# Tile 0's second product four blocks at a time, loads in order of first use, one more pair of chunks through the DMA crossbar

## The chip, the cores and the metric

The kernel runs on one core of one Trainium2 chip. The metric is the device time of one execution in microseconds (us). A core has five engines that run side by side, each through its own instructions in order: TensorE (PE) multiplies matrices into PSUM, VectorE (DVE) and ScalarE (ACT) work element by element, GpSimd (POOL) also does element work and here issues all loads, and SyncE (SP) issues stores and transposing DMAs. They wait for each other through semaphores.

## The reference

A linear attention with decay feeds a two-layer network with an ELU between its layers. Sizes: batch 4, 8 heads, sequence 768, head size 64; so x is 3072 x 512, w_in 512 x 2048, w_out 2048 x 512. Cut to what is computed:

```python
for b in range(nb):                      # blocks of 64 positions
    intra = (einsum(qb, kb) * Dmask) @ vb          # decay lam ** (i - j), i >= j
    inter = (qb * lam_pow) @ kv_state
    out[:, :, sl] = intra + inter
    kv_state = lam_block * kv_state + einsum(kb * rev_pow, vb)
x = out.transpose(0, 2, 1, 3).reshape(B * S, H * D)
h = x @ w_in
g = where(h > 0, h, exp(min(h, 0)) - 1)
return (g @ w_out).astype(float32)
```

## The kernel before

It works in chunks of 128 positions of one batch (24 chunks, numbered 0 to 23; 0 to 3 are the first positions of the four batches and have no state). Chunks come in pairs; each pair passes through three visits: transposes of q and k (`att_T`, on PE through PSUM with a copy by ACT, or `att_xT`, by a transposing DMA, the crossbar), scores and mask (`att_S`, `att_mask`), outputs and state (`att_O`, `att_U`, `att_X`, `att_st`). Chunks are gathered to seven tiles, of 4, 2, 4, 4, 4, 4 and 2 chunks, whose columns go through the network: `mm1` makes one of 16 blocks of 128 hidden units (PE into psH), ACT makes e and r of it, DVE makes g (`elu`), and `mm2` adds one hidden block's part to one output block of 128 rows (PE into psM).

```python
TS = [4, 2, 4, 4, 4, 4, 2]                 # chunks of each tile

LOADS = [(0, 1, 'q'), (0, 1, 'k'), (0, 1, 'v'), (1, 1, 'q'), ...,
         (2, 1, 'v'), (3, 1, 'v'), ('wi', 0), ('wi', 1), ('wi', 2), ...,
         ('kd', 0), ('wi', 6), ('kd', 2), ('wo', 0), (4, 2), ('wo', 1), ('wo', 2), ('wo', 3),
         (6, 2), (8, 2), (10, 2), ..., (22, 2)]      # issued by POOL, in this order

def att_T(g, n, which, tag="S"):           # transposes on PE
    ...
            nc.tensor.transpose(pt[:, i, hp, :], in_=nat[:, 2 * hp : 2 * hp + 2, :],
                                identity=ident16[:])

def att_xT(g):                             # transposes by DMA, issued by SP
    for j, ts in enumerate((qn, kn)):
        dst = asb.tile([128, 2 * HP, 128], FP16, tag=f"{w}T", name=f"{w}T{g}", bufs=3)
        nc.sync.dma_start_transpose(out=dst[:], in_=heads(ts, g, 2)...)

def att_st(g):
    ...
        if c == 0:
            copy = nc.scalar.copy if g in (2,) else nc.vector.tensor_copy
            copy(out=new[r, :, :, r], in_=pu[r])

def mm1(t, n, alt=False):                  # psH: 2 buffers of tag H (and M for tile 0, some n)
    ...
    e = msb.tile([128, MT], FP32, tag="e", bufs=3, ...)
    nc.scalar.activation(e[:], pH[:], AF.Exp)
    r = msb.tile([128, MT], FP16, tag="r", bufs=3, ...)
    nc.scalar.activation(r[:], pH[:], AF.Relu)

def mm2(t, i, n, tag="M"):                 # psM: 2 buffers of tag M; copied and stored at n = 15
    ...
    nc.tensor.matmul(pm[:], lhsT=gt[t][:, n, i * L : (i + 1) * L],
                     rhs=wo_t[...], start=(n == 0), stop=(n == NF - 1))
    ...
    nc.sync.dma_start(out=out[t0 : t0 + L, :], in_=o[:])
```

The order of all this is written out by hand. A list of steps says which hidden block is made in a step and which (tile, output block, hidden block) parts of mm2 follow it; visits of the attention are attached to steps. Within a step, mm1 comes first, then what is attached, then g, then mm2. Stage A is tile 0's 16 hidden blocks, stage B steps without a hidden block; later steps carry their tile and hidden block, and E is the end.

```python
steps = [(('A', 0), (0, 0), []), ..., (('A', 9), (0, 9), []),
         (('A', 10), (0, 10), [(0, 0, 0), (0, 1, 0)]), ...,
         (('B', 0), None, [(0, 0, 6), (0, 1, 6), (0, 0, 7), (0, 1, 7)]), ... to ('B', 4),
         ((1, 0), (1, 0), [(0, 2, 0), (0, 3, 0), (0, 2, 1), (0, 3, 1)]), ...,
         ((2, 0), (2, 0), [(1, 0, 0), (1, 0, 1)]), ...]
for s, m1, m2 in steps:
    if m1 is not None:
        t, n = m1
        er = mm1(t, n, alt=t == 0 and n in (2, 4, 6))
    do(s)                                  # what is attached to this step
    if er:
        elu(t, n, *er)
    for t2, i2, n2 in m2:
        mm2(t2, i2, n2, "H" if t2 == 0 and m1 is None and i2 > 1 else "M")
```

At the start, `warm(k)` puts k matmuls of 512 columns without use on PE between the first transposes.

Of the kernel before, what the change touches and what calls it, by code (L numbers as in the profile page):

```python
# [7 lines left out]
FP32 = mybir.dt.float32  # L8
FP16 = mybir.dt.float16
I32 = mybir.dt.int32  # L10
AF = mybir.ActivationFunctionType
# [4 lines left out]
def kernel(  # L16
# [10 lines left out]
    nc = tc.nc  # L27

    B, H, S, D = q.shape
    L = 128  # L30
    HP = H // 2
# [6 lines left out]
    T0 = [sum(TS[:t]) for t in range(len(TS))]  # L38
# [74 lines left out]
    LOADS = [(0, 1, 'q'), (0, 1, 'k'), (0, 1, 'v'), (1, 1, 'q'), (1, 1, 'k'), (1, 1, 'v'), (2, 1, 'q'), (2, 1, 'k'), (3, 1, 'q'), (3, 1, 'k'), (2, 1, 'v'), (3, 1, 'v'), ('wi', 0), ('wi', 1), ('wi', 2), ('wi', 3), ('wi', 4), ('wi', 5), ('kd', 0), ('wi', 6), ('kd', 2), ('wo', 0), (4, 2), ('wo', 1), ('wo', 2), ('wo', 3), (6, 2), (8, 2), (10, 2), (12, 2), (14, 2), (16, 2), (18, 2), (20, 2), (22, 2)]  # L113

    def run_loads(items):
        for it in items:
            if it[0] == "wi":
                emit_wi(it[1])
            elif it[0] == "wo":
                emit_wo(it[1])  # L120
            elif it[0] == "kd":
                att_kd(it[1], 2, "p")
            else:
                emit_load(*it)

    nc.gpsimd.iota(rel_i[:], pattern=[[1, 128]], base=0, channel_multiplier=-1)
    run_loads(LOADS[:17])
# [31 lines left out]
    for hh in range(2):  # L159
        nc.vector.tensor_tensor(  # L160
            out=mask1[:, hh],
# [20 lines left out]

    def late_up():
        nc.scalar.activation(ks[:], loglam[:], AF.Exp, scale=pos[:, 1:2])
        for hh in range(2):
            r = slice(hh * 64, (hh + 1) * 64)
            nc.scalar.copy(loglam_p[r, :], loglam[r, hh::2])
        nc.scalar.activation(up_p[:], loglam_p[:], AF.Exp, scale=float(L))

    def late_qs(lo, hi):  # L190
        for hp in range(lo, hi):
            nc.scalar.activation(
                qs[:, hp, :], row[:], AF.Exp, scale=loglam_p[:, hp : hp + 1]
            )
# [105 lines left out]
    def att_S(g, tag="S"):  # L300
        s = ps.tile([128, 2, HP, 128], FP32, tag=tag, bufs=2, name=f"psS{g}")
        for hp in range(HP):
            for hh in range(2):
                r = slice(hh * 64, (hh + 1) * 64)
                nc.tensor.matmul(  # L305
                    s[:, hh, hp, :], lhsT=kT[g][r, hp, :], rhs=qT[g][r, hp, :],
                    start=True, stop=True,
                )
        pS[g] = s
# [37 lines left out]
    def att_X(g, n, parts=1):  # L347
        t, i = where[g]
        if i == 0:
            xt[t] = asb.tile([128, HP, TS[t] * L], FP16, tag="xt", name=f"xt{t}")  # L350
        po = pS.pop(("O", g))
        w = HP // parts
        for j in range(parts):
            c = slice(j * w, (j + 1) * w)
            dst = xt[t][:, c, i * L : (i + n) * L].rearrange("p h (n l) -> p n h l", n=n)
            if g < B:
                copy = nc.vector.tensor_copy if g == 0 else nc.scalar.copy
                copy(out=dst, in_=po[:, :, c])
                continue
            nc.vector.tensor_tensor(  # L360
                out=dst, in0=po[:, :, c],
                in1=qs[:, c].unsqueeze(1).broadcast_to([128, n, w, 128]),
                op=ALU.mult,
            )
# [36 lines left out]
    def att_st(g):  # L401
        c, b = divmod(g, B)
        if c == NC - 1:
            return
        pu = pS.pop(("U", g))
        new = st[b // 2][(c + 1) % 2]
        for hh in range(2):
            r = slice(hh * 64, (hh + 1) * 64)
            if c == 0:
                copy = nc.scalar.copy if g in (2,) else nc.vector.tensor_copy  # L410
                copy(out=new[r, :, :, r], in_=pu[r])
            else:
                nc.vector.tensor_tensor(  # L413
                    out=new[r, :, :, r], in0=tmps[g][r], in1=pu[r], op=ALU.add
                )
        tmps.pop(g, None)
# [18 lines left out]
    def mm1(t, n, alt=False):  # L435

        MT = TS[t] * L
        if MT == 256:
            if n == 0:
                gt[t] = msb.tile([128, NF, MT], FP16, tag="g", bufs=2, name=f"g{t}")  # L440
            pH = ps.tile([128, 2 * MT], FP32, tag="H", bufs=2, name=f"psH{t}_{n}")
            for x in range(2):
                wi, j = wi_t[wi_at[n + x][0]], wi_at[n + x][1]
                for kk in range(HP):
                    nc.tensor.matmul(  # L445
                        pH[:, x * MT : (x + 1) * MT],
                        lhsT=wi[:, kk, j * 128 : (j + 1) * 128],
                        rhs=xt[t][:, kk, :], start=(kk == 0), stop=(kk == HP - 1),
                    )
            MT *= 2  # L450
        else:
            if (t, n) not in pH_of:
                mm1_mm(t, n, 0, MT, "M" if t == 0 and n % 2 == 0 and n < 8 else "H")
            pH = pH_of.pop((t, n))
        e = msb.tile([128, MT], FP32, tag="e", bufs=3, name=f"e{t}_{n}")
        nc.scalar.activation(e[:], pH[:], AF.Exp)  # L456
        if alt:
            return e, None, pH
        r = msb.tile([128, MT], FP16, tag="r", bufs=3, name=f"r{t}_{n}")
        nc.scalar.activation(r[:], pH[:], AF.Relu)  # L460
        return e, r, pH
# [35 lines left out]
    def mm2(t, i, n, tag="M"):  # L497
        if T0[t] + i == NG - 1:
            if n == NF - 1:
                mm2_last(t, i)  # L500
            return
        if n == 0:
            psM[t, i] = ps.tile([128, DM], FP32, tag=tag, bufs=2, name=f"psM{t}_{i}")
        pm = psM[t, i]
        nc.tensor.matmul(  # L505
            pm[:], lhsT=gt[t][:, n, i * L : (i + 1) * L],
            rhs=wo_t[wo_at[n][0]][:, wo_at[n][1], :], start=(n == 0), stop=(n == NF - 1),
        )
        if n < NF - 1:
            return  # L510
        c, b = divmod(T0[t] + i, B)
        t0 = b * S + c * L
        o = msb.tile([128, DM], FP32, tag="osb", bufs=3, name=f"osb{t}_{i}")
        last = T0[t] + i == NG - 1
        if last:
            raise AssertionError
        else:
            if i % 2:
                nc.vector.tensor_copy(o[:], pm[:])
            else:  # L520
                nc.scalar.copy(o[:], pm[:])  # L521
            nc.sync.dma_start(out=out[t0 : t0 + L, :], in_=o[:])
        psM.pop((t, i))

    def warm(k, tag="M"):
        if k <= 0:
            return
        pw = ps.tile([128, 4, 128], FP32, tag=tag, bufs=2, name=f"psW{len(warms)}")
        warms.append(pw)
        for _ in range(k):  # L530
            nc.tensor.matmul(
                pw[:], lhsT=ident16[:], rhs=any16, start=True, stop=True
            )
# [13 lines left out]
    def op_T(c, w):  # L547
        att_T(c, 1, w, "H")

    def op_Te(c, w):  # L550
        att_Te(c, 1, w, "a")

    W = [5, 2, 3, 0, 1, 1, 0, 0, 1, 1, 0]
# [7 lines left out]
    late_up()  # L561
    warm(W[2])
    att_S(0)
    att_mask(0, 2)
    warm(W[3])
    op_T(1, "q")
    op_Te(1, "q")
    warm(W[4])
    op_T(1, "k")
    op_Te(1, "k")  # L570
    att_O(0, 1, "M")
    att_X(0, 1)
    warm(W[5])
    att_S(1)
    att_mask(1, 2)
    op_T(2, "q")
    op_Te(2, "q")
    warm(W[6])
    op_T(2, "k")
    op_Te(2, "k")  # L580
    warm(W[7])
# [3 lines left out]
    att_mask(2, 2)  # L585
    att_O(1, 1, "M")
    att_X(1, 1)
    warm(W[8])
    att_T2(3, "k", "H")
    warm(W[9])  # L590
    att_S(3)
    att_mask(3, 2)
    att_O(2, 1, "M")
    att_X(2, 1)
    late_qs(0, 2)
    warm(W[10])
    for n in range(0):
        mm1_mm(0, n, 0, 3 * L, "MH"[n % 2])
    att_OX2(3, "H")
    for n in range(0, 1):  # L600
        mm1_mm(0, n, 0, 3 * L, "MH"[n % 2])
    late_qs(2, HP)
    for n in range(1):
        mm1_mm(0, n, 3 * L, 4 * L)

    run_loads(LOADS[17:27])
# [8 lines left out]
    XT = {10: (1, 12), 12: (2, 4), 14: (2, 12), 16: (3, 4), 18: (3, 12), 20: (4, 4), 22: (4, 12)}  # L615
# [23 lines left out]
    for g, vs in [(4, (('A', 12), ('A', 14), ('B', 1))), (6, ((1, 0), (1, 4), (1, 6))), (8, ((1, 8), (1, 12), (1, 14))), (10, ((2, 0), (2, 2), (2, 5))), (12, ((2, 8), (2, 10), (2, 13))), (14, ((3, 0), (3, 2), (3, 5))), (16, ((3, 8), (3, 10), (3, 13))), (18, ((4, 0), (4, 2), (4, 5))), (20, ((4, 8), (4, 10), (4, 13))), (22, ((5, 0), (5, 2), (5, 5)))]:  # L639
        visit(g, *vs)  # L640
    for s, a, b in [((1, 0), 27, 28), ((1, 4), 28, 29), ((1, 8), 29, 30), ((1, 12), 30, 31), ((2, 0), 31, 32), ((2, 3), 32, 33), ((2, 6), 33, 34), ((2, 9), 34, 35)]:
        at(s, run_loads, LOADS[a:b])

# [42 lines left out]
```

## Time and profile before

| | |
|---|---|
| Time, median of 3 runs | 216.54 us (216.33 to 216.77) |
| Span of the profiled run | 215.2 us |
| PE busy | 203.1 us, 94% |
| DVE busy | 151.0 us, 70% |
| ACT busy | 127.8 us, 59% |
| POOL busy | 79.0 us, 37% |
| DMA of loads (POOL's queue) | 13.63 MB |
| DMA of stores and transposes (SP's queue) | 9.90 MB |

Busy time of an engine is the time in which at least one of its instructions runs, and an idle piece before an instruction is put down to what released it. Matmuls overlap in the records, so a busy PE is not one at its peak: beside the busy time, the time from start to start of the same matmuls has to be read. DMA records give the time of each transfer's issue and of its landing.

### The profile page before, as it was taken

The numbers are of one execution on the slowest core, as the hardware profiler recorded it, in microseconds if no ns is written. First come the engines' busy times: TensorE is split into PE (matmuls) and PEld (weight loads), VectorE is DVE, ScalarE is ACT, GpSimd is POOL, SyncE is SP. The second block draws the span as 40 slices with busy tenths as digits, with TensorE's granted clock in tenths as the row PEclk, the third lists the DMA queues.
The fourth block names the chain that finished last, engine by engine and source line by source line (L and its number), as shares of the span: only waits on it lengthen the run. The fifth ranks groups of instructions, "written<-read, shape, count | busy, mean of one in ns | idle before, by whom it ended". The sixth has DMA issues, their size and how long they took to land.

```text
span 215.2 us, 4091 instructions
## 1 busy us (share of the span) xinstructions
PE 203.1 (94%) x1650; PEld 105.9 (49%) x1650; DVE 151.0 (70%) x193; ACT 127.8 (59%) x241; POOL 79.0 (37%) x76
## 2 busy tenths in 40 slices
PE   4977979899999999999999999999999999999994
PEld 1443434566764544544544545545445444555543
DVE  6666998985999999997887786766565543423221
ACT  6848888436566766676565566466456567454510
POOL 8999958469498948255400000000000000000000
DMA  6999999999999999999992413314211011111112
GB/s 40 146 157 169 206 171 195 191 162 150 157 126 156 206 138 168 135 156 177 184 153 74 75 49 86 63 49 98 53 49 52 0 49 49 53 49 49 49 51 99
DMA packets 98756, 23.87 MB, mean 111 GB/s; under 512 B 90928, under 2 KB 95792, under 8 KB 98736
## 3 DMA queue, kind: packets, MB, share of 16 engines
q0 software_dynamic: 80208, 13.63, 84.1%
q1 hardware_dynamic: 18384, 9.90, 21.6%
q8 instruction: 13, 0.21, 0.4%
q10 hardware_dynamic: 144, 0.07, 0.1%
q14 instruction: 7, 0.06, 0.1%
HBM read 27.27 MB, written 6.29 MB: 156 GB/s over the span
## 4 chain that ended last, share of the span: by engine, by line
PE 58%; POOL 17%; DMA 14%; issue 5%; DVE 4%; ACT 0%; POOLq 0%; DVEq 0%
PE psM L505 29%; PE psH L430 15%; PE psH L445 6%; DMA kT<-kn 5%; DMA qn<-in_q_dram 5%; DMA wo<-in_moe_w_out_dram 4%; POOL qn L72 3%; POOL kn L72 3%; POOL vn L72 3%; POOL tmp L394 3%; POOL wi L97 2%; DVE g L473 2%; PE psO L331 2%; POOL kd L292 2%; PE psM L485 2%
## 5 line engine op out<-in xcount | busy, mean ns | idle before, releaser
L473 DVE SCALAR_TENSOR_TENSOR g<-e,r 128x512 f16<-128x512 f32 x93 | 69.5, 761 | 41.7 <-ACT r L460 41.2
L456 ACT ACTIVATE e<-psH 128x512 f32<-128x512 f32 x96 | 57.5, 599 | 63.9 <-PE psH L430 48.4
L505 PE MATMUL psM<-wo,g 128*128 128x512 f16 x368 | 93.9, 380 | 1.0 <-DMA wo<-in_moe_w_out_dram 0.9
L430 PE MATMUL psH<-xt,wi 128*128 128x512 f16 (+2 forms) x324 | 81.2, 377 | 1.2 <-DMA wi<-in_moe_w_in_dram 0.8
L460 ACT ACTIVATE r<-psH 128x512 f16<-128x512 f32 x93 | 55.3, 595 | 0.0
L505 PEld LDWEIGHTS <-g 128*128 128x128 f16 x368 | 34.2, 98 | 38.7 <-DMA wo<-in_moe_w_out_dram 1.4
L430 PEld LDWEIGHTS <-wi 128*128 128x128 f16 x324 | 31.1, 98 | 38.9 <-DMA wi<-in_moe_w_in_dram 1.3
L317 DVE TENSOR_TENSOR P<-psS,mask 128x1024 f16<-128x1024 f32 (+1 forms) x28 | 28.7, 1066 | 4.0 <-PE psS L305 3.8
L394 POOL TENSOR_TENSOR tmp<-st,up_p 64x512 f32<-64x512 f16 x16 | 21.4, 1336 | 13.3 <-DVE st L413 12.5
L72 POOL DMA_DIRECT2D qn<-in_q_dram x14 | 15.8, 1125 | 5.1 <-issue 4.5
L72 POOL DMA_DIRECT2D vn<-in_v_dram x14 | 15.3, 1096 | 5.9 <-issue 4.9
L445 PE MATMUL psH<-xt,wi 128*128 128x256 f16 x128 | 16.6, 273 | 0.0
L72 POOL DMA_DIRECT2D kn<-in_k_dram x14 | 15.3, 1092 | 3.0 <-issue 1.8
L360 DVE TENSOR_TENSOR xt<-psO,qs 128x1024 f16<-128x1024 f32 x10 | 12.2, 1221 | 4.9 <-PE psO L339 4.7
L445 PEld LDWEIGHTS <-wi 128*128 128x128 f16 x128 | 12.5, 98 | 4.9
L521 ACT COPY osb<-psM 128x512 f32<-128x512 f32 x12 | 7.1, 590 | 11.8 <-PE psM L505 11.8
L331 PE MATMUL psO<-P,vn 128*64 128x128 f16 x184 | 11.9, 223 | 0.8 <-DVE P L317 0.8
L292 DVE TENSOR_TENSOR kd<-kn,ks 128x1024 f16<-128x1024 f16 x8 | 12.4, 1549 | 0.0
L331 PEld LDWEIGHTS <-vn 128*64 128x64 f16 x184 | 9.6, 109 | 5.1 <-issue 4.4
L413 DVE TENSOR_TENSOR st<-tmp,psU 64x512 f16<-64x512 f32 x16 | 10.9, 679 | 0.2
L339 PE MATMUL psO<-qT,st 128*64 128x128 f16 x160 | 10.2, 219 | 0.0
L305 PE MATMUL psS<-qT,kT 64*128 64x128 f16 x192 | 8.2, 221 | 0.9 <-DMA kT<-kn 0.7
(62 smaller groups left out, 106.4 us busy)
## 6 DMA issues: line engine op xcount, KB each, us to landing
out_dram<-osb SPq DMA_DIRECT2D x23, 256.0 KB, 2.3
qn<-in_q_dram POOLq DMA_DIRECT2D x10, 256.0 KB, 12.2
kn<-in_k_dram POOLq DMA_DIRECT2D x10, 256.0 KB, 14.8
vn<-in_v_dram POOLq DMA_DIRECT2D x10, 256.0 KB, 15.7
wo<-in_moe_w_out_dram POOLq DMA_DIRECT2D x4, 512.0 KB, 13.6
wi<-in_moe_w_in_dram POOLq DMA_DIRECT2D x2, 512.0 KB, 9.6
wi<-in_moe_w_in_dram POOLq DMA_DIRECT2D x3, 256.0 KB, 7.3
qn<-in_q_dram POOLq DMA_DIRECT2D x4, 128.0 KB, 4.5
```

What stands on the lines that cost most here:

```text
L72: nc.gpsimd.dma_start(out=dst, in_=src[b : b + n, :, rows].rearrange("b h p d -> p (b h) d"))
L292: e.tensor_tensor(out=kd[:].rearrange("p (n h) d -> p n h d", n=n), in0=heads(kn, g, n).rearrange("p (n h) d -> p n h d", n=n), in1=ks_b, ...
L317: nc.vector.tensor_tensor(out=P[:, :, c], in0=s[:, :, c], in1=(mask if g < B else mask1)[:, :, c], op=ALU.mult,)
L331: nc.tensor.matmul(po[r, i, hp, :], lhsT=v_of(g + i, 2 * hp + hh), rhs=P[:, hh, hp, :], start=True, stop=(c == 0), skip_group_check=True,)
L360: nc.vector.tensor_tensor(out=dst, in0=po[:, :, c], in1=qs[:, c].unsqueeze(1).broadcast_to([128, n, w, 128]), op=ALU.mult,)
L394: e.tensor_tensor(out=tmp[r], in0=old[r, :, :, r], in1=up_p[r].unsqueeze(1).unsqueeze(3).broadcast_to([64, 2, HP, 64]), op=ALU.mult,)
L430: nc.tensor.matmul(pH[:, lo:hi], lhsT=wi[:, kk, j * 128 : (j + 1) * 128], rhs=xt[t][:, kk, lo:hi], start=(kk == 0), stop=(kk == HP - 1),)
L445: nc.tensor.matmul(pH[:, x * MT : (x + 1) * MT], lhsT=wi[:, kk, j * 128 : (j + 1) * 128], rhs=xt[t][:, kk, :], start=(kk == 0), stop=(kk = ...
L456: nc.scalar.activation(e[:], pH[:], AF.Exp)
L460: nc.scalar.activation(r[:], pH[:], AF.Relu)
L473: nc.vector.scalar_tensor_tensor(out=g, in0=e[:], scalar=-1.0, in1=r[:], op0=ALU.add, op1=ALU.min)
L505: nc.tensor.matmul(pm[:], lhsT=gt[t][:, n, i * L : (i + 1) * L], rhs=wo_t[wo_at[n][0]][:, wo_at[n][1], :], start=(n == 0), stop=(n == NF - 1),
```

## The change

It rearranges the schedule; what is computed stays the same.

- Loads of the first four chunks: q and k of all four come ahead of their v. Chunks 4 and 5 come behind the second piece of wo rather than behind the first.
- mm2 of tile 0 runs four output blocks at once in a longer stage B (steps B0 to B13), so that each piece of wo serves four blocks while the next is loaded. Two of the blocks use PSUM buffers of tag H. mm2 of tiles 1 to 5 is spread anew: it begins within its own tile's hidden blocks.
- Chunks 8 and 9 are transposed by the DMA crossbar and no longer by PE. Visits of chunks 4 to 9 and four of the load issues move to other steps.
- The first chunks' transposes are put in another order with the other early work, with more but shorter warm-up matmuls (256 columns).
- State casts of pair 2 go from ACT to DVE, the first output's cast from DVE to ACT.
- Stores of output blocks 18 and 19 are issued by POOL instead of SP.

The diff, cut to its core (`...` marks cuts):

```diff
-    LOADS = [(0, 1, 'q'), (0, 1, 'k'), (0, 1, 'v'), (1, 1, 'q'), ..., ('wi', 4), ('wi', 5), ('kd', 0), ('wi', 6), ('kd', 2), ('wo', 0), (4, 2), ('wo', 1), ('wo', 2), ('wo', 3), (6, 2), ...]
+    LOADS = [(0, 1, 'q'), (0, 1, 'k'), (1, 1, 'q'), (1, 1, 'k'), (2, 1, 'q'), (2, 1, 'k'), (3, 1, 'q'), (3, 1, 'k'), (0, 1, 'v'), (1, 1, 'v'), (2, 1, 'v'), (3, 1, 'v'), ('wi', 0), ..., ('wi', 3), ('kd', 0), ('wi', 4), ('wi', 5), ('kd', 2), ('wi', 6), ('wo', 0), ('wo', 1), (4, 2), ('wo', 2), ('wo', 3), (6, 2), ...]
...
-                copy = nc.vector.tensor_copy if g == 0 else nc.scalar.copy
+                copy = nc.vector.tensor_copy if g in () else nc.scalar.copy
...
-                copy = nc.scalar.copy if g in (2,) else nc.vector.tensor_copy
+                copy = nc.scalar.copy if g in () else nc.vector.tensor_copy
...
+                [128, 2 * MT], FP32, tag="M" if (t, n) in ((1, 0),) else "H", bufs=2,
...
-            nc.sync.dma_start(out=out[t0 : t0 + L, :], in_=o[:])
+            (nc.gpsimd if T0[t] + i in (18, 19) else nc.sync).dma_start(
+                out=out[t0 : t0 + L, :], in_=o[:]
+            )
...
-                pw[:], lhsT=ident16[:], rhs=any16, start=True, stop=True
+                pw[:, 0:2], lhsT=ident16[:], rhs=any16[:, 0:2], start=True, stop=True
...
-    W = [5, 2, 3, 0, 1, 1, 0, 0, 1, 1, 0]
+    W = [10, 4, 3, 1, 2, 1, 2, 1, 3, 2, 2, 3]
... (the first chunks' transposes, scores and outputs in another order)
-    XT = {10: (1, 12), 12: (2, 4), ...}
+    XT = {8: ('B', 13), 10: (1, 12), 12: (2, 4), ...}
...
-    for g, vs in [(4, (('A', 12), ('A', 14), ('B', 1))), (6, ((1, 0), (1, 4), (1, 6))), (8, ((1, 8), (1, 12), (1, 14))), (10, ...
+    for g, vs in [(4, (('B', 1), ('B', 4), ('B', 7))), (6, (('B', 12), (1, 0), (1, 4))), (8, ((1, 6), (1, 10), (1, 14))), (10, ...
...
-    for s, a, b in [((1, 0), 27, 28), ((1, 4), 28, 29), ((1, 8), 29, 30), ...
+    for s, a, b in [(('B', 2), 27, 28), (('B', 5), 28, 29), (('B', 8), 29, 30), ...
...
-    steps = [..., (('A', 10), (0, 10), [(0, 0, 0), (0, 1, 0)]), ..., (('B', 0), None, [(0, 0, 6), (0, 1, 6), (0, 0, 7), (0, 1, 7)]), ..., ((2, 0), (2, 0), [(1, 0, 0), (1, 0, 1)]), ..., ((3, 0), (3, 0), [(2, 0, 0), (2, 0, 1), (2, 0, 2), (2, 0, 3)]), ...
+    steps = [..., (('A', 12), (0, 12), [(0, 0, 0), (0, 1, 0)]), ..., (('B', 0), None, [(0, 2, 0), (0, 2, 1), (0, 2, 2), (0, 2, 3)]), ..., (('B', 2), None, [(0, 0, 4), (0, 1, 4), (0, 2, 4), (0, 3, 4)]), ... to ('B', 13), ((1, 0), (1, 0), []), ..., ((1, 6), (1, 6), [(1, 0, 0), (1, 1, 0), (1, 0, 1), (1, 1, 1)]), ..., ((2, 5), (2, 5), [(1, 1, 15), (2, 0, 0), (2, 0, 1)]), ..., ((3, 0), (3, 0), [(2, 0, 13), (2, 1, 8), (2, 0, 14), (2, 1, 9)]), ...
```

## What was predicted

> **What bounds the kernel now.** I read, in this order: the page, for shares; busy time by stretch, for where TensorE (PE) idles; PE's timeline, for what ends each idle piece; then the timelines of ACT, DVE and SyncE (SP) around those pieces. The first table (stretch, length, PE busy with its count, clock, DMA share, GB/s):
>
> ```profile
> 20.16:39.75 19.59, 17.77 (x133) 1.00 1.56 193
> 39.75:66.10 26.35, 25.79 (x325) 1.00 1.90 153
> 66.10:112.00 45.90, 45.18 (x372) 1.00 2.07 166
> 112.00:212.30 100.30, 100.18 (x700) 1.00 0.20 56
> ```
>
> The reader is to see that from 20 us on PE idles 1.82 + 0.56 + 0.72 + 0.12 = 3.22 us in all, nearly all of it before 42 us, and that DMA traffic is heavy until 112 us and light after. Which waits these are, PE's timeline says (start, length, tile, idle time before it in brackets):
>
> ```profile
> 20.16 3.63 PE L430 MATMUL psH<-xt,wi 128*128 128x512 f16 x16 [0.78 <-DMA wi<-in_moe_w_in_dram]
> ...
> 28.51 1.02 PE L430 MATMUL psH<-xt,wi 128*128 128x512 f16 x4 [0.31 <-ACT r L460]
> 30.45 0.61 PE L505 MATMUL psM<-wo,g 128*128 128x512 f16 x2 [0.92 <-DMA wo<-in_moe_w_out_dram]
> ...
> 34.17 0.62 PE L218 MATMUL psT<-ident,kn 128*128 128x128 f16 x8 [0.50 <-DMA kn<-in_k_dram]
> ...
> 41.80 0.25 PE L331 MATMUL psO<-P,vn 128*64 128x128 f16 x2 [0.47 <-DVE P L317]
> ...
> 82.48 0.62 PE L305 MATMUL psS<-qT,kT 64*128 64x128 f16 x16 [0.35 <-DMA kT<-kn]
> 112.02 0.62 PE L305 MATMUL psS<-qT,kT 64*128 64x128 f16 x16 [0.38 <-DMA kT<-kn]
> ```
>
> So the kernel is fed by loads up to about 43 us, and is PE throughput after. Two things matter below. The third weight piece of wi lands just before 20.16, and nothing that PE does earlier can start the hidden layer's third block sooner. And the two late waits are for transposed keys that the DMA crossbar makes just in time.
>
> **What the Trainium skill says.** "TensorE: Matmul & The Clock Gate", Part 1, section "Wait — 56ns, not 53.3ns?", gives 215.7 ns from start to start of warm 512-column matmuls; four of them take 0.86 to 0.87 us in the chain, 216 ns each, so I count PE work with 0.216. "DMA: Bandwidth & Descriptors", section "Issuing engines are not separate DMA queues", says that DMAs from all engines run on the same 16 DMA engines and interleave. The trace agrees: from 56 to 59 us loads alone move 156 GB/s; while one crossbar pair runs, from 60 to 66 us, all queues together average 133, and in a quarter of that time the slices show under 20. "PSUM — Partial Sum Buffer", Specifications (TRN2), gives eight banks of 512 fp32 values; the four output blocks of tile 0 therefore need four, both M and both H buffers, which are free in stage B because no hidden block is computed there.
>
> **The change part by part.**
>
> *Loads in order of first use.* q and k of all four first chunks come ahead of v. The 12 pieces and the wi pieces behind them are the same bytes on the same queue, so wi's third piece still lands at about 20.1 us. The reordering lets the first transposes run earlier, but PE then idles longer before 20.1. Worth on the path: 0. The smaller warm-up matmuls lie in the same hole: 0.
>
> *wo waits and mm2 order.* Before, mm2 of tile 0 begins at step A10, and PE, which runs in order, stands 0.92 us for wo. After, mm2 begins at A12, when wo's first piece is there (30.4 us, if it lands as before), and chunk 4 is transposed in stage B, behind the weights, without the 0.50 wait. Stage B then has 56 mm2 matmuls, four blocks for each wo row block, instead of 20, so masking on DVE (2.3 us for two chunks) hides and the 0.47 goes too. With the 0.08 before one mm2: saved 0.92 + 0.50 + 0.08 + 0.47 = 1.97 us.
>
> *Casts of the state move from ACT to DVE.* In the kernel before ACT does one pair at 28.34 (1.18 us) and DVE one at 26.83:
>
> ```profile
> 26.83 1.40 DVE L411 CAST st<-psU 64x512 f16<-64x512 f32 x2
> 28.26 0.43 DVE L468 TENSOR_SCALAR m<-e 128x512 f16<-128x512 f32 x1
> 28.72 0.69 DVE L471 TENSOR_TENSOR g<-m,psH 128x512 f16<-128x512 f16 x1
> 29.32 2.03 DVE L473 SCALAR_TENSOR_TENSOR g<-e,r 128x512 f16<-128x512 f32 x3
> ```
>
> After, another 1.40 lies between g of block 7 and g of block 8. Going forward with 0.61 per g, 0.48 between starts of ACT's e and r, and three e buffers: g7 ends 29.95, casts 31.35, g8 31.95; e of block 11 needs e8's buffer, so it starts at 31.95 and its r ends at 32.95. Hidden block 13 on PE needs that PSUM bank, and starts at 32.95 instead of about 32.25: 0.7 us lost. The same rule gives about 0.6 on block 12, of which 0.31 stands before already. Net loss 1.0. With A12 to A15 at 1.30 us (four mm1, two mm2) stage A ends at 36.85.
>
> *Stage B by sum from there.* 56 mm2 x 0.216 = 12.1; chunks 4-5 and 6-7 transposed, 2 x 0.89 = 1.8; scores 0.65; outputs and state 1.37: 15.9, so tile 1 starts at 52.8. What remains for PE: 320 mm1 + 320 mm2 of 512 columns = 138.4; nine pairs of scores at 0.66 = 5.9; seven output pairs with state at 1.37 and two without at 1.12 = 11.8. Sum 156.1, so PE ends at 208.9 without any wait. Before it ends at 212.2, and its tail to the end of the span is 2.95, which does not change. Span without waits: 211.9, 3.3 less. In this sum are the 0.89 us of PE transposes of chunks 8-9, which the crossbar takes over, and the late waits.
>
> *The crossbar pair for chunks 8-9* is the dear part. These lines are SP's timeline (start, time of issue):
>
> ```profile
> 58.72 1.33 SPq L274 DMA_TRANSPOSE qT<-qn  x1
> 60.48 1.78 SPq L274 DMA_TRANSPOSE kT<-kn  x1
> 66.44 2.94 SPq L522 DMA_DIRECT2D out_dram<-osb  x2
> 69.48 2.05 SPq L274 DMA_TRANSPOSE qT<-qn  x1
> 71.63 4.65 SPq L274 DMA_TRANSPOSE kT<-kn  x1
> ```
>
> The keys of 60.48 landed 8.2 us later, those of 71.63 10.8 us later, by the trace's issue and landing times: a pair needs about 10 us from its first issue. In the kernel before, POOL issued the loads of chunk 8 at 46.84 because it waited 4.37 us for DVE's state before; the queue ran dry for about 3 us. After, those loads precede that operation and land at about 50 and 52 us. The pair is issued behind two stores at about 51, and its keys land at 61 to 63. Its scores stand at step (1,10): 52.8 + 9.0 = 61.8. Expected wait 0.6. The pair also costs loads about 4 us (from 60 to 66 they moved 0.26 MB instead of 0.94), against 3 gained by the earlier issue and with four stores in the way instead of two; the keys of chunks 10-11, which landed at 68.7, land at about 72, and their scores are due at 71.5. Expected wait 0.5 more. Later pairs stay as near to their use as before: I keep 0.4.
>
> *Two stores on POOL* (blocks 18 and 19): near 190 us, where POOL and DMA idle: 0.
>
> **Sum.** 211.9 + 0.6 + 0.5 + 0.4 = 213.4, that is 1.8 us under 215.2. I take that difference off the median of 216.54: **214.7 us**, a gain of 0.8%.
>
> **The rivals.**
>
> *A: the new order closes all holes.* Then the gain is at most the 3.22 us of idle time after 20.16 less the 0.1 of the last stretch, plus 0.89: 4.0 us, 212.5. For it: most of the waits after 20.16 lie where the diff moves something. Against it: the DVE casts and the new crossbar pair each make a wait. Over 2% would need more than 4.3 us, which is more than there is, unless wi lands sooner or bubbles too short to show vanish too; about 1.2 us of these lie between counted work and busy time.
>
> *B: the crossbar becomes the bound from 50 to 112 us.* One pair more in a DMA stream that was full there makes every later pair late, by up to 2 us each, until the loads end. For it: 0.35 and 0.38 of wait already. Against it: mm2 matmuls of tiles 2 and 3 are moved ahead of later scores, about 20 of them, 4.3 us, which gives the transposes time. It would make the time 216 to 218.
>
> *C: DVE sets the pace in tile 2.* It is busy 7.97 of 8 us from 80 to 88 in the kernel before, and mm2 of tile 2 now follows its own g by about three steps where it followed by a whole tile. A late g would now stop PE. Against it: PSUM and e buffers keep PE within a few blocks of DVE anyway. Cost 0 to 2 us.
>
> **Range and chances.** The plain sum is 213.4 of span; A takes off 2 at most, B and C add up to 3. The range is 212.6 to 216.8. Faster by over 2% means under 212.2, below A's best: 0.05. Slower by over 2% needs B and C together: 0.04. Within 2%: 0.91.
>
> **What would show each step right or wrong.** Right: no PE wait for wo and none for kn at 30 to 35 us; PE still waits for wi at about 20; PE waits of some tenths for ACT r or DVE g between 28 and 36; tile 1's first matmul near 53; a wait of PE for kT near 62 or 72. Wrong: if wi's third piece lands well before 20, the whole schedule moves and I am too slow; if no kT wait shows up, the gain is nearer 3 us; if PE waits for DVE's g in tile 2 or for kT at each pair, the time is at or over 216.5.

## The result and the profile after

The changed kernel takes 219.09 us (median of 4 runs, 218.64 to 220.07) against 216.44 for the kernel before; the ratio is 1.013, 95% interval 1.009 to 1.017. It is slower, by about 1.3%, and the predicted 214.7 us (212.6 to 216.8) was wrong. The profiled run has a span of 216.8 us; times are 1.7 to 1.9 us above spans in these two profiles and in those of the experiments.

First, PE's busy time by stretch, cut at the same points of the work as in the prediction: wi's third piece, the end of stage A, tile 2's first matmul, 112 us, the last matmul (stretch, length, PE busy with its count, clock, DMA share, GB/s):

```profile
19.38:36.00 16.62, 15.46 (x97) 1.00 1.49 179
36.00:71.33 35.33, 33.00 (x365) 0.95 2.00 174
71.33:112.00 40.67, 39.23 (x345) 1.00 2.31 162
112.00:213.90 101.90, 101.90 (x709) 1.00 0.24 59
```

Idle time in them is 1.16 + 2.33 + 1.44 + 0 = 4.93 us, against 3.22 before. It shrank in stage A, where the change meant to save, from 1.82 to 1.16, and grew behind it; and for the first time the clock column of a stretch is under 1.00. PE's timeline has two pieces that make up most of it:

```profile
53.41 1.05 PE L450 MATMUL psH<-xt,wi 128*128 128x256 f16 x8
56.70 1.65 PE L450 MATMUL psH<-xt,wi 128*128 128x256 f16 x7 [2.23 <-DVE osb L524]
...
89.16 0.62 PE L307 MATMUL psS<-qT,kT 64*128 64x128 f16 x16 [1.31 <-DMA kT<-kn]
```

The first stands in tile 1, at its third pair of hidden blocks, in a place where the kernel before has no wait at all. What held DVE is on DVE's timeline:

```profile
50.20 2.08 DVE L294 TENSOR_TENSOR kd<-kn,ks 128x1024 f16<-128x1024 f16 x1
55.95 0.69 DVE L524 COPY osb<-psM 128x512 f32<-128x512 f32 x1 [3.67 <-DMA out_dram<-osb]
```

Four output blocks are now finished within 3 us, and there are three buffers `osb` to copy them to. The copy of the fourth waits until the first's store has landed; until then its PSUM bank of tag H is not free, and the third pair of hidden blocks on PE needs that bank. The view of tile osb around there gives the stores' times, issue to landing, 6.0 and 6.7 us for the first two:

```profile
L527 SPq DMA_DIRECT2D out_dram<-osb x2: 342/385/428, 49.9 to 50.3; - x2
...
DMA to landing us min/median/max: 6.0/6.3/6.7
```

In the kernel before, the same two stores took 4.2 and 4.4 us. There, the loads of chunk 8 were issued only together with them, at 46.84; here those loads were issued from 41.57 on and are in flight ahead of them. "DMA: Bandwidth & Descriptors", section "Issuing engines are not separate DMA queues", in the Trainium skill says that transfers of all queues interleave on the same engines; the slower stores agree with it, though no run here separates the loads' share.

The second wait, at 89 us, starts in the order of SP's instructions:

```profile
49.87 0.82 SPq L527 DMA_DIRECT2D out_dram<-osb  x2
52.27 1.42 SPq L276 DMA_TRANSPOSE qT<-qn  x1
54.02 3.99 SPq L276 DMA_TRANSPOSE kT<-kn  x1
58.05 1.12 SPq L527 DMA_DIRECT2D out_dram<-osb  x2
59.61 2.99 SPq L276 DMA_TRANSPOSE qT<-qn  x1
63.88 3.29 SPq L276 DMA_TRANSPOSE kT<-kn  x1
76.70 0.33 SPq L527 DMA_DIRECT2D out_dram<-osb  x1
77.14 1.38 SPq L276 DMA_TRANSPOSE qT<-qn  x1
78.60 4.73 SPq L276 DMA_TRANSPOSE kT<-kn  x1
```

SP issues in order. The pair of chunks 12 and 13 (77.14 and 78.60) stands behind the store of tile 1's first block (76.70), which the new spread of mm2 finishes at step (2,2). Its keys landed 10.5 us after their issue, by the view of tile kT, and their scores stand six steps later, at (2,10). In the kernel before, this pair was issued at 69.48 and 71.63, 13 us ahead of its use.

Last, the clock after the first wait, from the same view in finer stretches:

```profile
54.00:56.00 2.00, 0.46 (x5) 1.00 1.41 258
56.00:58.00 2.00, 1.30 (x7) 0.59 2.03 172
58.00:60.00 2.00, 2.00 (x37) 0.56 1.61 157
60.00:62.00 2.00, 2.00 (x34) 1.00 1.71 141
```

From 56 to 60 us PE had (0.41 + 0.44) x 2 = 1.7 us less of full clock. What that cost is not read off so easily: three of the four runs, the profiled one among them, have a mean clock of 0.992, and the fourth has 1.000 and took 218.93 us, no less than the others' 218.64 to 220.07.

### The profile page after: what moved, and what is told of

The parts are those of the page before. It is cut to its first block, busy times and chain, and to the rows that moved or that the text cites. A ratio compares the mean times of both kernels' runs of the same rounds, so it can differ in the third digit from the quotient of the medians.

```text
span 216.8 us, 4093 instructions
## 1 busy us (share of the span) xinstructions
PE 204.1 (94%) x1650; PEld 107.5 (50%) x1650; DVE 149.2 (69%) x193; ACT 126.3 (58%) x238; POOL 78.8 (36%) x78
## 4 chain that ended last, share of the span: by engine, by line
PE 76%; DMA 11%; POOL 8%; ACT 1%; DVE 1%; issue 1%; SPq 0%; DVEq 0%; POOLq 0%; ACTq 0%
PE psM L510 35%; PE psH L432 25%; PE psH L450 6%; DMA kT<-kn 5%; DMA wi<-in_moe_w_in_dram 4%; DMA out_dram<-osb 3%; PE psO L333 3%; PE psS L307 2%; PE psO L341 2%; POOL wi L97 2%; POOL qn L72 2%; POOL kn L72 2%; PE psM L490 2%; POOL vn L72 2%; POOL kd L294 1%
## 5 line engine op out<-in xcount | busy, mean ns | idle before, releaser
L432 PE MATMUL psH<-xt,wi 128*128 128x512 f16 x320 | 81.3, 379 | 2.2 <-DMA wi<-in_moe_w_in_dram 0.9
L527 POOL DMA_DIRECT2D out_dram<-osb x2 | 1.2, 594 | 83.6 <-ACT osb L526 79.6
L396 POOL TENSOR_TENSOR tmp<-st,up_p 64x512 f32<-64x512 f16 x16 | 20.0, 1247 | 8.8 <-DVE st L415 7.8
L450 PE MATMUL psH<-xt,wi 128*128 128x256 f16 x128 | 17.4, 282 | 2.2 <-DVE osb L524 2.2
L524 DVE COPY osb<-psM 128x512 f32<-128x512 f32 x11 | 7.6, 687 | 5.9 <-DMA out_dram<-osb 3.7
L294 DVE TENSOR_TENSOR kd<-kn,ks 128x1024 f16<-128x1024 f16 x8 | 11.4, 1431 | 0.0
L415 DVE TENSOR_TENSOR st<-tmp,psU 64x512 f16<-64x512 f32 x16 | 10.9, 681 | 0.2
## 6 DMA issues: line engine op xcount, KB each, us to landing
qn<-in_q_dram POOLq DMA_DIRECT2D x10, 256.0 KB, 15.9
```

The costliest lines, as they stand in the source:

```text
L294: e.tensor_tensor(out=kd[:].rearrange("p (n h) d -> p n h d", n=n), in0=heads(kn, g, n).rearrange("p (n h) d -> p n h d", n=n), in1=ks_b, ...
L396: e.tensor_tensor(out=tmp[r], in0=old[r, :, :, r], in1=up_p[r].unsqueeze(1).unsqueeze(3).broadcast_to([64, 2, HP, 64]), op=ALU.mult,)
L432: nc.tensor.matmul(pH[:, lo:hi], lhsT=wi[:, kk, j * 128 : (j + 1) * 128], rhs=xt[t][:, kk, lo:hi], start=(kk == 0), stop=(kk == HP - 1),)
L450: nc.tensor.matmul(pH[:, x * MT : (x + 1) * MT], lhsT=wi[:, kk, j * 128 : (j + 1) * 128], rhs=xt[t][:, kk, :], start=(kk == 0), stop=(kk = ...
```

## The experiments

The theory to start with: the store that holds the buffer (S). The rival: the new crossbar pair (X). Each edit is against the changed kernel unless said otherwise.

### e1: the fourth block gets memory of its own

The fourth block's copy goes to memory of the first chunks' mask, which nobody reads any more.

```diff
-        o = msb.tile([128, DM], FP32, tag="osb", bufs=3, name=f"osb{t}_{i}")
+        if (t, i) == (0, 3):
+            o = mask[:, 0].rearrange("p h l -> p (h l)")
+        else:
+            o = msb.tile([128, DM], FP32, tag="osb", bufs=3, name=f"osb{t}_{i}")[:]
```

> The changed kernel, but the fourth output block of tile 0 is copied into memory of the first chunks' mask, which nobody reads any more, instead of into the osb buffer that the first block's store still holds. Theory S (store holds the buffer): PE's wait of 2.23 us for DVE's osb near 55 us is gone, TensorE's clock stays at 1.00 from 50 to 60 us, and the time falls by 2.2 us for the wait plus about 1.4 us for the slow clock after it, from 219.1 to about 215.5. Rival X (the new crossbar pair fills the DMA engines): the wait for osb goes, but PE is then stopped at the scores of chunk 8, whose keys land at about 64 us, and at chunk 12 by more than the present 1.31 us; time 217 to 218.5.

Measured: 221.5 us, ratio 1.025 (1.019 to 1.031). The wait for osb is gone and the kernel is slower. PE's timeline:

```profile
64.67 1.04 PE L307 MATMUL psS<-qT,kT 64*128 64x128 f16 x16 [3.39 <-DMA kT<-kn]
```

These are the scores of chunk 8. PE reached them at 61.28, as the prediction had it (61.8), and their keys landed at 64.6: issued at 52.8, they took 11.8 us. Chunk 12's scores then wait for 1.90 us (1.31 in the changed kernel). So the wait for osb was there, but taking it away only brings PE sooner to a key that is not there. Theory S fails as the whole cause, and X had the place right but the size too small: in the profiled run two spells of half clock follow the two waits. The runs with one such spell, by their mean clock of 0.992, took 220.3 and 220.6 us, those with two (0.985) 222.4 and 223.1.

### e2: chunks 8 and 9 transposed by PE again

```diff
-    XT = {8: ('B', 13), 10: (1, 12), 12: (2, 4), ...}
+    XT = {10: (1, 12), 12: (2, 4), ...}
```

> The changed kernel, but chunks 8 and 9 are transposed by PE again, so one crossbar pair less. Theory S: the first store is issued ahead of that pair and waits behind loads, so its landing moves little, PE's wait for osb near 55 us stays at 1.5 us or more, with the slow clock; PE has 0.89 us more work; time 218 to 219.5. Rival X: without the pair the stores land some 2 us earlier, PE's wait for osb falls under 0.5 us, the wait of 1.31 us for the keys of chunk 12 goes too; time 215 to 216.

Measured: 223.35 us, ratio 1.035 (1.030 to 1.040): a miss for both. The wait for osb stays, 2.13 us, so the pair doesn't cause it (S right). But it is 4.3 us slower than the changed kernel, of which PE's transposes are 0.89. Chunk 12's keys, now free of one pair ahead of them, are awaited for 3.14 us instead of 1.31; they are issued at 79.47, behind the same store. Shorter new waits near 59, 61 and 102 us come to 1.30; the rest was not taken apart. One pair more in the DMA stream is thus not needed to make them late; their place in SP's order is a candidate, which e4 tests.

### e3: PE's hole filled in part

```diff
+            if m1 == (1, 4):
+                warm(10)
             er = mm1(t, n, alt=t == 0 and n in (2, 4, 6))
```

> The changed kernel with 20 halves of warm-up work, that is 10 matmuls of 256 columns (1.1 us at full clock), put into PE's hole ahead of step (1,4); the wait for the buffer stays. Theory S with the clock as a cost of its own: the matmuls fill about half of the hole, the rest of it is too short for the clock to fall, the records show 1.00 from 56 to 60 us, and the time falls by about 1.4 us, to 217.7. Rival: the clock is a mere sign of the hole; the time stays at 219 within 0.4.

Measured: 218.94 us, ratio 1.013 (1.010 to 1.016), as the changed kernel, which is the rival's number. The clock stays at 1.00 in all four runs. But in the profiled one chunk 12's keys are awaited for 1.75 us instead of 1.31, and waits that the edit does not touch differ by about as much as was to be seen (1.04 us for chunk 4's keys, where the changed kernel has none, and 1.18 for wi, where it has 0.41). It doesn't decide on the clock, because whatever is saved before 89 us can be taken back there. e8 asks again.

### e4: the pair of chunks 12 and 13 ahead of the store

```diff
-    XT = {8: ('B', 13), 10: (1, 12), 12: (2, 4), ...}
+    XT = {8: ('B', 13), 10: (1, 12), 12: (2, 1), ...}
```

> The changed kernel, but the crossbar pair of chunks 12 and 13 stands at step (2,1) in SyncE's order, ahead of the store of the first block of tile 1 (end of step (2,2)), instead of at (2,4), behind it. Theory S holds that the wait of 1.31 us for these keys at 89 us comes from that order: the pair is issued at about 75 us when its keys are loaded, lands at about 85, and the wait is gone; time 1.0 to 1.3 us less, 217.9. Rival X (a full DMA stream makes each pair late): the pair lands at 87 or later in spite of its earlier issue, and the waits of later pairs grow; time within 0.4 of 219.1.

Measured: 217.67 us, ratio 1.0075 (1.0055 to 1.0096), 1.4 us less than the changed kernel (1.2 by the ratios). The clock is not behind it: with a mean clock of 0.992 the runs took 217.9 and 218.3 against 218.6 to 220.1 there, and with 1.000 both took 217.5 against 218.9. SP's timeline shows the order and the issue, 5.2 us earlier for the queries and 4.3 for the keys:

```profile
71.96 1.24 SPq L276 DMA_TRANSPOSE qT<-qn  x1
74.33 3.72 SPq L276 DMA_TRANSPOSE kT<-kn  x1
78.15 0.59 SPq L527 DMA_DIRECT2D out_dram<-osb  x1
```

The keys still take 9.8 us but are there in time, and no wait for them is left. A transposed key is late here by its issue, not by a slower transfer.

### e5: both moves

The edits of e1 and e4 together:

```diff
+        if (t, i) == (0, 3):
+            o = mask[:, 0].rearrange("p h l -> p (h l)")
...
-    XT = {8: ('B', 13), 10: (1, 12), 12: (2, 4), ...}
+    XT = {8: ('B', 13), 10: (1, 12), 12: (2, 1), ...}
```

> The changed kernel with both moves: the fourth output block's own memory, and the crossbar pair of chunks 12 and 13 ahead of tile 1's first store. Theory now (each transposed key lands at a time that SyncE's order and the loads set, and PE is stopped by whichever comes last): no wait for osb, none for the keys of chunk 12, but the wait of 3.4 us for the keys of chunk 8 near 64.7 us stays, because these still land at 64.6; time 217.5 to 218.5, no better than with pair 12 moved alone (217.67). Rival (waits simply add up): the time falls by the 2.2 us of the osb wait against that run, to 215.5.

Measured: 219.46 us, ratio 1.014 (1.009 to 1.018), above the range that the theory gave. As it had it, the waits don't add up: without the wait for osb, PE waits for chunk 8's keys, which landed at 65.1:

```profile
65.17 0.62 PE L307 MATMUL psS<-qT,kT 64*128 64x128 f16 x16 [3.03 <-DMA kT<-kn]
```

It is even slower than e4, by 1.8 us (1.3 by the ratios). In e4, whose hole lay earlier, PE came to these scores at 64.1, just after the keys had landed at 63.7, and in its profile the clock stayed up; here it falls.

### e6: both moves, chunks 8 and 9 by PE

e5, and

```diff
-    XT = {8: ('B', 13), 10: (1, 12), 12: (2, 1), ...}
+    XT = {10: (1, 12), 12: (2, 1), ...}
```

> As the kernel with both moves, and chunks 8 and 9 transposed by PE again, as in the kernel before. Theory: nothing is left that stops PE for more than 0.6 us after 35 us; the gains that were predicted for the load order and the four output blocks come out, the 0.89 us for PE's transposes is paid: 214.3 to 215.5, below the kernel before (216.15). Rival (the new spread of mm2 or stage B itself costs time): 216 or more.

Measured: 216.26 us, ratio 0.9989 (0.997 to 1.0006), no difference from the kernel before. All the new waits are gone. The profile, with a span of 213.7, has one PE wait over 0.1 us after 36 us, of 0.46:

```profile
36.00:70.00 34.00, 33.42 (x385) 1.00 2.05 180
70.00:112.00 42.00, 42.00 (x361) 1.00 2.05 161
```

Taking the waits away thus brings 2.8 us, from 219.09 down, though PE makes the transposes again. But the median is above what I expected (214.3 to 215.5) and in the rival's range, and the 0.7 to 1.9 us that were to be gained on the kernel before are not there. The profile flatters: its run took 215.5 us, 0.8 under the median, while the profiled run of the kernel before (216.93) lay above its own. Both kernels spread alike from run to run (215.3 to 217.2 here, 215.5 to 217.6 before), and what makes the spread stayed open. That stage B or the new spread of mm2 costs some time of its own is not excluded.

### e7: the pair of chunks 8 and 9 made first

Both moves, and the keys come earlier in both queues:

```diff
-    LOADS = [..., ('wo', 3), (6, 2), (8, 2), (10, 2), ...]
+    LOADS = [..., ('wo', 3), (6, 2, 'qk'), (8, 2), (10, 2), ...]
-    XT = {8: ('B', 13), ...}
+    XT = {8: ('B', 9), ...}
-        at(s, run_loads, LOADS[a:b])
+        at(s, run_loads, [(8, 2, 'qk'), (6, 2, 'v'), (8, 2, 'v')] if a == 27 else LOADS[a:b])
```

> As the kernel with both moves, but the crossbar pair of chunks 8 and 9 stays and is made early: q and k of chunks 8 and 9 are loaded ahead of v of chunks 6 to 9, and the pair stands ahead of tile 0's stores in SyncE's order. Theory: the keys are loaded at about 51 us, transposed at about 60.5, the scores are due at 61.3, so no wait over 0.5 us; 0.9 us better than with PE transposes: 213.5 to 215. Rival (the pair as such fills the DMA engines, and its cost comes back at chunks 10 or 12): PE waits of 1 us or more at 72 or 88 us; 215.5 to 217.

Measured: 214.95 us, ratio 0.992 (0.990 to 0.995): faster than both kernels, by 0.8% than the one before. Two of its five runs took 219.59 and 220.56 us, at a mean clock of 0.992, and are left out of the ratio as slow; the median of the other three is 214.72, and what those two waited for is not on record. In the profiled run the keys land at 60.3; the one late key is chunk 10's, 0.44 us at 72 us, where the prediction had 0.5. No wait of 1 us or more comes, as the rival would have it: made early, the pair is hidden.

### b1: that pair alone, in the kernel before

```diff
-    XT = {10: (1, 12), 12: (2, 4), ...}
+    XT = {8: (1, 4), 10: (1, 12), 12: (2, 4), ...}
```

> The kernel before, with nothing changed but that chunks 8 and 9 are transposed by the crossbar (at step (1,4)) instead of by PE. Theory: q and k of chunk 8 are loaded at 53 and 55 us there, so the pair lands at about 64, the scores are due at 61.3 less nothing, PE waits some 2.5 us, saves 0.89 us, and later pairs come 3 us later, so that PE waits at them too: 217.5 to 219. Rival (the pair is hidden, and only the other parts of the change cost): 215.3 to 216.3.

Measured: 224.0 us, ratio 1.037 (1.032 to 1.042), the highest median of all. Ahead, PE's timeline; then SP's:

```profile
65.84 1.03 PE L305 MATMUL psS<-qT,kT 64*128 64x128 f16 x16 [5.95 <-DMA kT<-kn]
```

```profile
53.07 1.35 SPq L274 DMA_TRANSPOSE qT<-qn  x1
54.95 3.21 SPq L274 DMA_TRANSPOSE kT<-kn  x1
58.54 2.45 SPq L274 DMA_TRANSPOSE qT<-qn  x1
63.38 1.83 SPq L274 DMA_TRANSPOSE kT<-kn  x1
```

The keys of 54.95 took 10.9 us and PE stood at their scores from 59.9. The clock records show half clock for 6.8 us after it, which costs 3.4 more. This one pair, put alone into the kernel before, costs 7.6 us. It is not quite the diff's pair, which stands at the end of stage B and whose keys are loaded sooner; here they landed only just ahead of its issue. The expected 217.5 to 219 had the wait too short and no clock in it.

### e8: the wait in e5 filled

```diff
+        if g == 8:
+            at(s1, warm, 28, "S")
         at(s1, att_S, g)
```

> The kernel with both moves (fourth block's own memory, pair 12 early), in which PE waits 3.03 us for the keys of chunk 8 and then works at half clock for some 3.3 us. Now 28 matmuls of 256 columns without use (3.0 us at full clock) stand ahead of these scores; the keys land no sooner. Theory (the half clock after a long wait costs by itself): the clock stays at 1.00 from 60 to 72 us, and the time falls by half of 3.3 us, to 217.5 to 218. Rival (only the wait counts; or the work put in delays the scores): 219 or more.

Measured: 217.86 us, ratio 1.008 (1.005 to 1.010), 1.6 us less than e5 (1.3 by the ratios, just clear of noise with four runs each), with the scores at the same 65.17. First e5, then e8, the clock in the fourth column:

```profile
62.00:64.00 2.00, 0.14 (x2) 1.00 2.19 77
64.00:66.00 2.00, 0.83 (x18) 0.98 1.45 276
66.00:68.00 2.00, 2.00 (x8) 0.50 1.54 167
68.00:70.00 2.00, 2.00 (x10) 0.67 1.61 156
```

```profile
62.00:64.00 2.00, 2.00 (x21) 1.00 1.64 76
64.00:66.00 2.00, 1.73 (x27) 1.00 1.53 283
66.00:68.00 2.00, 2.00 (x15) 1.00 1.54 171
68.00:70.00 2.00, 2.00 (x37) 1.00 2.13 155
```

Work of no use in the hole, and the kernel is faster. In e5 the half clock takes (0.50 + 0.33) x 2 = 1.7 us of full clock on top of the wait of 3 us, and about that much comes back.

### e9: keys of chunks 10 and 11 ahead of v of 8 and 9, too

```diff
-        at(s, run_loads, [(8, 2, 'qk'), (6, 2, 'v'), (8, 2, 'v')] if a == 27 else LOADS[a:b])
+        at(s, run_loads, {27: [(8, 2, 'qk'), (6, 2, 'v'), (10, 2, 'qk'), (8, 2, 'v')],
+                          28: [(10, 2, 'v')]}.get(a, LOADS[a:b]))
```

> As the kernel with pair 8 made first (214.95), and q and k of chunks 10 and 11 are now also loaded ahead of v of chunks 8 and 9. Theory (each pair's landing is its keys' landing plus about 10 us): these keys land about 1.8 us sooner, the wait of 0.44 us at 72 us is gone; 214.2 to 215, with less spread from run to run. Rival (the loads only change places, something else is then late): 215 to 216.

Measured: 214.75 us, ratio 0.992 (0.990 to 0.994), the lowest of all and not told from e7. One run of 22 took 217.5 us, the others 213.3 to 216.4. The loaded keys of chunk 10 landed even 3.5 us sooner than in e7, at 58.6 instead of 62.1, but their transposed form was no sooner: 71.8 instead of 72.0, and the wait is 0.37 us instead of 0.44. SP's timeline tells why, with the pair of chunk 8 now ahead of the four stores:

```profile
49.89 1.34 SPq L276 DMA_TRANSPOSE qT<-qn  x1
51.73 3.67 SPq L276 DMA_TRANSPOSE kT<-kn  x1
55.46 1.67 SPq L530 DMA_DIRECT2D out_dram<-osb  x3
57.18 0.47 SPq L530 DMA_DIRECT2D out_dram<-mask  x1
57.74 3.86 SPq L276 DMA_TRANSPOSE qT<-qn  x1
```

SP itself was busy with issuing the queries' transpose of chunk 10 from 57.74 to 61.60, and issued that of the keys at 61.70. A landing plus about 10 us, as I had it, is thus only half the rule; SP must be free as well.

### e10: e4 with chunks 8 and 9 by PE

As e6, without e1's edit:

```diff
-    XT = {8: ('B', 13), 10: (1, 12), 12: (2, 4), ...}
+    XT = {10: (1, 12), 12: (2, 1), ...}
```

> The changed kernel with pair 12 early and chunks 8 and 9 transposed by PE, but the fourth output block still in the shared osb buffers. With it the two causes up to 65 us can be told apart: theory says that here the osb wait of about 2.1 us is paid in full, since no key of chunk 8 hides it: 218.2 to 219, against 216.26 with the fourth block's own memory. Rival (the osb wait is never on the path): 216.3 within 0.4.

Measured: 220.48 us, ratio 1.019 (1.017 to 1.021). Against e6, which differs in the fourth block's memory alone, 4.2 us. The wait is back:

```profile
56.67 1.03 PE L450 MATMUL psH<-xt,wi 128*128 128x256 f16 x8 [2.21 <-DVE osb L524]
```

In this profile a spell of half clock follows, 1.7 us, and one more wait of 0.84 for a g near 100 us. More than expected, since that had no clock in it. But 1.7 is not a fixed price: two of the four runs, at mean clocks of 0.996 and 0.997, can have lost only about 0.9 us of clock (0.004 of 219 us) and took 220.6 all the same. In e4 (217.67) the same wait costs little, since without it PE waits for chunk 8's keys (e5).

### e11: e9 with the state cast of pair 2 on ACT again

```diff
-                copy = nc.scalar.copy if g in () else nc.vector.tensor_copy
+                copy = nc.scalar.copy if g in (2,) else nc.vector.tensor_copy
```

> As the best kernel so far (keys first, 214.75), with one part of the change undone: the state cast of pair 2 is made by ACT again, as in the kernel before. It tests the term of the prediction that charged this move with a net 1.0 us at hidden blocks 12 and 13. If the term is right, 213.7 to 214.2. If not (PE's waits for ACT's r between 28 and 33 us were 0.4 us more than before in the changed kernel, and ACT is delayed by 1.18 us in turn), within 0.4 of 214.75.

Measured: 215.32 us, ratio 0.996 (0.993 to 0.998), against 0.992 for e9, and above both forecasts. PE's timeline, first e9's, then this one's:

```profile
30.93 1.02 PE L432 MATMUL psH<-xt,wi 128*128 128x512 f16 x4 [0.19 <-ACT r L465]
```

```profile
30.02 1.36 PE L432 MATMUL psH<-xt,wi 128*128 128x512 f16 x5 [1.15 <-ACT r L465]
```

The cast costs PE a wait on ACT, not on DVE. The term of the prediction is refuted: the move doesn't lose a microsecond, and seems to gain about half of one.

## Why the prediction was wrong

*The sum from tile 1's start: the step that failed first.* It let 156.1 us of work run without waits other than for keys. It looked for PSUM banks in stage B and for when each copy's engine is free, and did not ask what the copy writes to. Four blocks at once need four osb buffers, there are three, and the first is held until a store has landed: PE waits 2.23 us. From 51.9: 156.1 + 2.95 gives 210.9; the waits of 2.23, 1.31, 0.13 and 0.10 give 214.7; the half clock 1.7 more, 216.4, with 0.4 of the measured 216.8 left unexplained. Between spans the miss is 216.8 - 213.4 = 3.4 us. Between medians it is 4.4, because the profiled run of the kernel before lay 0.5 above its median and that of the changed kernel 0.5 below.

*wo waits and stage B: the waits went, the times came out in part by luck.* No wait for wo or for chunk 4's keys is left in the changed kernel's profile. Stage A ended at 36.0 (predicted 36.85), tile 1 began at 51.9 (52.8); stage B took 15.9 us, as predicted. The 0.9 is nearly all in wi's third piece, whose block began at 19.38 instead of 20.16. The prediction had held that time fixed, and nothing shows this to be the change's doing: in e1, with the same loads, the block began at 20.18, and in b1, with the loads of the kernel before, PE did not wait for that piece at all. From that block on stage A took 16.62 us against a predicted 16.69, but with a new wait of 0.41 for a later piece of wi, which made up for a charge for the casts that was too high. And the 1.97 us to be saved were read from one profile: in b1, the same kernel up to 53 us, these waits came to 0.36 + 0.25 + 0.49 = 1.10.

*DVE casts: the chain was there, the charge was wrong.* ACT's e of block 11 waited 0.62 us for DVE's g and started at 30.97, 11.6 us behind the third block's start (predicted 11.8). PE was charged with 1.0 us for it; its waits for ACT's r came to 0.75, of which 0.31 was there before, and e11 shows that the cast is better off where the change put it.

*The crossbar pair for chunks 8-9: right mechanism, size off.* The term was a wait of 0.6 us. In the changed kernel it showed as none, because the hole before it hid it; with that closed it was 3.0 and 3.4 us (e5, e1). The scores' time was right to 0.5 us. The keys' landing was not: 63.9 in the changed kernel, 64.6 and 65.1 in e1 and e5, instead of 61 to 63, since q and k of chunk 8 landed at 52 and 54, not at 50 and 52, and the keys' transfer took 9.9 to 11.8 us, where the prediction had seen 8.2 and 10.8.

*"Later pairs stay as near to their use as before: I keep 0.4"* failed too: 1.31. I had noted that the spread of mm2 moves later scores back and gives the transposes time (against rival B). But it also moves tile 1's first store ahead of a pair in SP's order, which held the pair back (e4).

*Two terms were missing altogether:* the clock after a wait, and that waits hide each other. The rival that came nearest is B, by its kind and its bound from 50 to 90 us, though not by its reason, one pair more in the stream: with a pair less the keys were later (e2), and issued earlier they were in time (e4, e7). The load traffic has its part all the same. While loads run, the keys took 8.2 to 11.8 us in the lines above; in the kernel before, from 118 us on, when the loads are done, 3.1 to 3.2. Rival C did not come: PE does not wait for a g in the changed kernel's tile 2.

What became of the expected gain: the changed kernel lost 2.8 us to one wait for a buffer, one for a key, and a clock spell (e6). Without them, but with PE's transposes, it is only level with the kernel before. With the pairs and their loads issued early as well, and a fourth place to copy to, the change is worth 0.8% (e9), which is the predicted number by a kernel that was not the predicted one.

## What to carry to other kernels

When a stage finishes more blocks at once, count every buffer on the way out, down to the store's landing, and not just the PSUM banks. A transfer that takes 10 us is placed by when it can be issued: look for what stands ahead of it in its issuing engine's order and for when its own input lands, before moving more work to it. And test a wait's cost by taking away the wait behind it as well, since the next one may be hidden under it.

## What the runs showed of the hardware that I had not expected

A wait of PE of 2 to 3 us can cost up to 1.7 us more in clock (e5 against e8). "TensorE: Matmul & The Clock Gate", Part 1, in the Trainium skill gives a free-running window of 3413 ns, and half clock after an idle window. The clock records agree with the length: each spell of half clock behind a wait lasted 3.41 us, and the one after b1's wait of 5.95 us 6.83, two of these. But no whole window of idleness was needed: the waits of 2.23 us (changed kernel) and 2.21 (e10) set a spell off, and those of 2.16 (e4), of 2.13 and even of 3.14 (e2) did not.

Where a wait falls on the window's grid accounts for these. Within each profile the changes of the clock lie whole multiples of 3.413 us apart, so the grid can be counted on from the start of its first clock record. A spell began behind windows in which PE had waited for 1.88 us (changed kernel), 1.90 and 3.23 (e1), 2.12 (e10), 2.66 (e5) and 3.41 (b1). The grid cut e2's wait of 3.14 into 1.90 + 1.24, its 2.13 into 1.72 + 0.41, and e4's 2.16 into 1.42 + 0.74, and no spell came. In these profiles the line thus lies near 1.9 us of waiting within one window. It doesn't explain b1's second window at half clock, since the one ahead of it held only 1.06 us of waiting; and no run was made to place a wait on the grid.
